# Moving three x-tile transposes behind first-piece products in the hand-written order of a 2:4-sparse linear layer

## The chip, the cores and the metric

One core of one Trainium2 chip runs the kernel. The metric is device time in microseconds (us) of one execution; lower is better. Four executions of the kernel before were timed, one of them under the profiler.

## What is computed

`x` has 16 x 512 tokens of 1024 features, `w` is 1024 x 1024, `b` has 1024 values, all bf16. The rows of `w` stand in groups of four; in each group and column the two largest magnitudes are kept and the rest set to zero. The pruned matrix multiplies all tokens, and the bias is added:

```python
    wg = w.reshape(G, M, D)
    mag = jnp.abs(wg)
    order = jnp.argsort(mag, 1)
    thr = jnp.take_along_axis(mag, order[:, M - N:M - N + 1, :], 1)
    mask = (mag >= thr)
    wp = (wg * mask).reshape(D, D)
    return jnp.einsum("bsd,df->bsf", x, wp) + b
```

## The kernel before

The 8192 tokens are 64 tiles of 128. TensorE (PE) needs, for every product, a 128 x 128 block of x with features on the partitions as weights, and up to 512 columns of the pruned matrix as the moving operand. Pruning takes VectorE (DVE) some 25 us, and the kernel is arranged so that PE has work from the first pruned columns on.

The weights are cut into six pieces (line 127): pieces 0 to 3 are 256 columns each of the upper half of the rows (g = 0), pieces 4 and 5 are 512 columns each of the lower half. In `w_sb` and `wp`, partition q holds the four rows of group q, so pruning a group is arithmetic within a partition.

The first eight tiles (0 to 7, `NPK`) use this layout as it is. Their first 512 features are loaded plainly (`load_x`, lines 116 to 122), transposed on PE with a stride of four (`transpose`, line 186), copied from PSUM to SBUF by ScalarE (ACT; `copy_xt`, line 194), and multiplied with a piece as soon as it is pruned (`mm_piece`, line 206). Two tiles of a pair (line 202) share one PSUM bank of 512 columns for each piece. When both are done, ACT copies the bank to SBUF (`stage`, line 253). Transposes rotate through two PSUM buffers (`psum_t`), partial sums through six (`psum_o`).

For everything else the pruned rows are brought back to their natural order by DMAs from `wp` to `wp_nat` (`spread`, line 141), and x arrives already transposed by transposing DMAs: `load_lead` (tiles 8 to 11), `load_low` (the second 512 features of tiles 0 to 7) and `load_nat` (all later tiles in batches). From then on PE runs products of 512 columns to the end, DVE adds the bias and ACT issues the stores.

The order of this first phase is written out by hand, one queue of tokens for each engine (`order`, line 259). A token is emitted when the tokens it needs are emitted (`needs`, `run`), and `seq` makes each engine keep the written order. So the strings in `order` are the instruction order of the engines. The tokens that matter here:

- `T3a` on PE: the four transposes of x tile 3 into a PSUM buffer (line 191, groups named `tp<-ident,x`). It wants the load of its tile and, for its buffer, the copy of the transpose two before it.
- `C3a` on ACT: the copy of that buffer to SBUF (line 196, `xt<-tp`).
- `M3.0y` on PE: the two products of tile 3 with piece 0 for the second half of the group rows (`x`: first half), line 217, `ps<-wp,xt`. Each has 256 columns. It wants `C3a` and the pruning token `mult0y`. Digits after the point are the piece.
- `S0b0` on ACT: the copy of pair 0's bank of piece 0 to `staged` (line 257, `st<-ps`). It frees a `psum_o` buffer. Pair 0 is tiles 5 and 6, pair 1 is 0 and 1, pair 2 is 2 and 3, pair 3 is 4 and 7.
- `W0.1` on SP: the DMAs that spread the pruned columns 512 to 1023 of g = 0 (line 100, `wp_nat<-wp`). `X0`, `X1`: the transposing DMAs of `xlead`.
- `A2h1` on PE: the first four products of tile 10 with columns 512 to 1023 (line 240, `ps<-wp_nat,xlead`), which want `W0.1`.

The loads of x are issued in this order: tile 7 by ACT, then by SP tiles 5 and 6, tiles 0 and 1, piece 1 of the weights, tile 4, tiles 2 and 3, and the rest of the weights. Tiles 2 and 3 are one transfer of 256 KB:

```python
    load_x(5, 7)
    load_x(0, 2)
    load_w(0, 256, 512)
    load_x(4, 5)
    load_x(2, 4)
    load_w(0, 512, 1024)
```

Of the kernel before, what the change touches and what calls it, by code (L numbers as in the profile page):

```python
# [10 lines left out]
def kernel(  # L11
# [241 lines left out]
    def stage(q, n):  # L253
        if (q, n // 2) not in staged:
# [3 lines left out]

    order = {
        "pe": (  # L260
            "F8 T7a T5a T6a T1a M5.0x M7.0x T0a M6.0x M6.0y M1.0x M7.0y M5.0y T3a M0.0y T4a M1.0y "
            "M0.0x T2a M3.0y M4.0x M3.0x M4.0y M2.0y M2.0x M4.1x M5.1x M0.1x M7.1y M6.1y M2.1y "
            "M1.1y M3.1y M6.1x M4.1y M1.1x M3.1x M0.1y M7.1x M2.1x M5.1y M0.2 M3.2 M7.2 M1.2 M2.2 "
            "M4.2 M6.2 M0.3 M2.3 M5.3 M4.3 M5.2 M6.3 M3.3 M1.3 A0h0 A2h0 M7.3 A2h1 A1h0 A3h1 A0h1 "
            "A3h0 A1h1"
        ),
        "dve": (
            "abs0a hi0a abs0b lo0a hi0b lo0b t20 t10 thr0 mask0x mult0x mask0y mult0y abs1 lo1 hi1 "
# [2 lines left out]
            "thr5 mask5 mult5"  # L271
        ),
        "act": (
            "C7a C5a C6a C1a C0a C3a C4a S0b0 C2a S3b0 S1b0 S2b0 abs3 S3b1 S1b1 S0b1 S2b1 S2b2 S1b2 "
            "S3b2 S0b2 S1b3 S2b3 W1.0q S3b3 S0b3"
        ),
        "sp": (
# [213 lines left out]
```

## Time and profile before

| | |
|---|---|
| median of the four runs | 233.75 us (233.69, 233.74, 233.76, 234.49) |
| the profiled execution | 234.49 us, of which 232.7 us is the span from first to last instruction |
| PE busy | 226.9 us, 98% of the span |
| granted clock of TensorE | 1.0 |
| transposes of x on PE (L191) | 32, 3.0 us busy |
| products of the first eight tiles with pieces 0 to 3 (L217) | 128 of 256 columns, 15.0 us busy |
| copies of transposes on ACT (L196) | 8, 0.37 us each |

The span is counted from the first instruction; times in the trace are microseconds from there. A product's recorded time (0.27 us for 256 columns) is longer than the distance to the next one, since products are pipelined. An entry such as `x4` stands for that many instructions in a row, and the bracket at the end of a line gives the idle time of the engine before it and what ended it.

### The profile page before, as it was taken

To read this page: it belongs to the slowest core of one execution; us is meant where nothing else is said; L and a number is where in the kernel's file an instruction comes from. 1 tells how busy PE (TensorE), PEld (TensorE's weight loads), DVE (VectorE), ACT (ScalarE), POOL (GpSimd) and SP (SyncE) were. 2 spreads that over 40 slices of the span, in tenths; PEclk is the share of its full clock that TensorE was granted. 3 is DMA by queue.
4 is the path that set the end of the run, shared out by engine and by line. 5 is a ranking of instruction groups with operands and counts; after the bars stand their busy time and mean duration, and the time that the engine had idled before them with its cause. 6 is when DMAs were issued, how large, how long until landed. Compare 5 with 4: busy or idle time off the path is not lost.

```text
span 232.7 us, 2829 instructions
## 1 busy us (share of the span) xinstructions
PE 226.9 (98%) x1139; PEld 112.5 (48%) x1158; DVE 108.2 (47%) x185; ACT 13.6 (6%) x27; POOL 17.6 (8%) x15
## 2 busy tenths in 40 slices
PE   8899999999999999999999999999999999999995
PEld 5688444554444444444444444444444444444443
DVE  4899858863244244234334334324324424423434
ACT  2575200000000000000000000000000000000000
POOL 1000099800000000000000000000000000000000
PEclk9999999999999999999999999999999999999999
DMA  6999999996389411992239921695228951122122
GB/s 190 300 217 227 218 183 258 310 248 236 148 186 243 157 68 70 231 285 73 90 88 216 282 92 46 155 270 162 93 90 179 238 169 68 70 90 79 60 90 90
DMA packets 78268, 38.19 MB, mean 164 GB/s; under 512 B 63664, under 2 KB 70576, under 8 KB 78256
## 3 DMA queue, kind: packets, MB, share of 16 engines
q1 hardware_dynamic: 67600, 20.88, 45.1%
q10 hardware_dynamic: 10656, 17.14, 20.7%
q8 instruction: 9, 0.15, 0.3%
q14 instruction: 3, 0.02, 0.0%
HBM read 3.41 MB, written 16.78 MB: 87 GB/s over the span
## 4 chain that ended last, share of the span: by engine, by line
PE 94%; DMA 2%; SPq 1%; issue 1%; DVE 0%
PE ps L240 87%; PE ps L217 5%; DMA x<-in_x_dram 2%; PE tp L240 1%; SPq L100 1%; PE tp L191 0%; DVE o L400 0%
## 5 line engine op out<-in xcount | busy, mean ns | idle before, releaser
L240 PE MATMUL ps<-wp_nat,xb 128*128 128x512 bf16 (+2 forms) x832 | 178.9, 375 | 0.8
L240 PEld LDWEIGHTS <-xb 128*128 128x128 bf16 x848 | 82.4, 98 | 97.5
L400 DVE TENSOR_TENSOR o<-ps,bias_sb 128x512 bf16<-128x512 f32 (+1 forms) x112 | 71.6, 677 | 114.6 <-PE ps L240 112.3
L396 POOL TENSOR_TENSOR st<-st,bias_sb 128x1024 f32<-128x1024 f32 x8 | 16.7, 2128 | 0.0
L217 PE MATMUL ps<-wp,xt 128*128 128x256 bf16 x128 | 15.0, 273 | 0.0
L240 PE MATMUL ps<-wp_nat,xlow 128*128 128x512 bf16 x62 | 14.0, 379 | 0.1
L217 PEld LDWEIGHTS <-xt 128*128 128x128 bf16 x128 | 12.3, 98 | 1.5
L402 DVE TENSOR_TENSOR o<-ps,st 128x512 bf16<-128x512 f32 x16 | 11.1, 692 | 2.8 <-PE ps L240 2.1
L240 PE MATMUL ps<-wp_nat,xlead 128*128 128x512 bf16 x47 | 11.1, 379 | 0.1
L240 PEld LDWEIGHTS <-xlow 128*128 128x128 bf16 x64 | 7.2, 112 | 6.7
L240 PEld LDWEIGHTS <-xlead 128*128 128x128 bf16 x64 | 6.3, 98 | 7.1
L257 ACT COPY st<-ps 128x512 f32<-128x512 f32 x16 | 8.5, 593 | 6.0 <-PE ps L217 4.2
L156 DVE TENSOR_TENSOR wp<-w_sb,mag 128x512 bf16<-128x512 bf16 (+2 forms) x8 | 5.4, 691 | 0.2
L156 DVE TENSOR_TENSOR mag<-mag,hi 128x512 bf16<-128x512 bf16 (+2 forms) x8 | 5.4, 690 | 0.2
L135 PE MATMUL ps<-zeros 128*128 128x128 bf16 (+1 forms) x22 | 4.2, 379 | 1.0 <-DVE zeros L86 1.0
L191 PE MATMUL tp<-ident,x 128*128 128x128 bf16 x32 | 3.0, 222 | 1.2 <-DMA x<-in_x_dram 0.9
L240 PE MATMUL tp<-wp_nat,xlead 128*128 128x512 bf16 x16 | 4.1, 379 | 0.0
L166 DVE TENSOR_SCALAR mag<-w_sb 128x512 uint16<-128x512 uint16 (+2 forms) x6 | 2.7, 467 | 2.7 <-DMA w_sb<-in_w_dram 2.7
L135 PEld LDWEIGHTS <-zeros 128*128 128x128 bf16 x22 | 2.4, 140 | 2.6 <-issue 1.6
L156 DVE TENSOR_TENSOR hi<-mag 128x512 bf16<-128x512 bf16 (+2 forms) x7 | 3.2, 460 | 0.1
L156 DVE TENSOR_TENSOR lo<-mag 128x512 bf16<-128x512 bf16 (+2 forms) x7 | 3.2, 458 | 0.0
L191 PEld LDWEIGHTS <-x 128*128 128x128 bf16 x32 | 2.3, 116 | 1.8 <-DMA x<-in_x_dram 1.4
(16 smaller groups left out, 14.0 us busy)
## 6 DMA issues: line engine op xcount, KB each, us to landing
out_dram<-o ACTq DMA_DIRECT2D x59, 256.0 KB, 2.8
wp_nat<-wp SPq DMA_DIRECT2D x14, 128.0 KB, 3.5
w_sb<-in_w_dram SPq DMA_DIRECT2D x3, 512.0 KB, 7.4
out_dram<-o ACTq DMA_DIRECT2D x8, 128.0 KB, 1.7
x<-in_x_dram SPq DMA_DIRECT2D x3, 256.0 KB, 4.2
w_sb<-in_w_dram SPq DMA_DIRECT2D x1, 256.0 KB, 4.6
bias_sb<-in_b_dram SPq DMA_DIRECT2D x1, 256.0 KB, 7.4
wp_nat<-wp ACTq DMA_DIRECT2D x2, 128.0 KB, 4.0
```

What stands on the lines that cost most here:

```text
L100: return seq(eng, q.dma_start(out_, in_))
L135: pe(nc.tensor.matmul(warm_ps[:, :rep * P], lhsT=zeros[:], rhs=zeros[:, None, :].to_broadcast([P, rep, P]), start=True, stop=True))
L156: dve(nc.vector.tensor_tensor(out, a, b_, op=op))
L166: dve(nc.vector.tensor_single_scalar(self.mag[:, ms, :].bitcast(u16), self.w[:, ms, :].bitcast(u16), 0x7FFF, op=Alu.bitwise_and))
L191: pe(nc.tensor.transpose(tp[:, m, :], xg[:, m, :], ident[:]))
L217: pe(nc.tensor.matmul(ps[:, c0 + d:c1 + d], lhsT=xpk[t][:, m, :], rhs=wp[:, g, m, c0:c1], start=(new and m == ms.start), stop=(left[(q, n) ...
L240: pe(nc.tensor.matmul(ps, lhsT=xt[:, kt - koff, :], rhs=wp_nat[:, kt, c0:c1], start=(kt == first), stop=(kt == last)))
L257: act(nc.scalar.copy(st[:, n % 2, :, :].rearrange("p t c -> p (t c)"), ps_open.pop((q, n))[:]))
L396: pool(nc.gpsimd.tensor_tensor(st[:], st[:], bias[:, :, None, :].to_broadcast([P, 2, 2, CW]), op=Alu.add))
L400: dve(nc.vector.tensor_tensor(o[:, c0:c1], ps, bias_sb[:, c0:c1], op=Alu.add))
L402: dve(nc.vector.tensor_tensor(o[:, c0:c1].rearrange("p (n c) -> p n c", n=2), ps.rearrange("p (n c) -> p n c", n=2), add, op=Alu.add))
```

## The change

Only the order of tokens changes, in the PE and the ACT queue. On PE, after `M5.0y`, the order `T3a M0.0y T4a M1.0y M0.0x T2a M3.0y M4.0x M3.0x M4.0y` becomes `M1.0y M0.0x T4a M0.0y M4.0x M4.0y T3a T2a M3.0y M3.0x`. On ACT, the copies of tiles 4 and 3 change places with the transposes, and `S0b0` goes behind `C2a`. The instructions themselves, and the queues of DVE, SP and GpSimd, are the same.

```diff
         "pe": (
-            "F8 T7a T5a T6a T1a M5.0x M7.0x T0a M6.0x M6.0y M1.0x M7.0y M5.0y T3a M0.0y T4a M1.0y "
-            "M0.0x T2a M3.0y M4.0x M3.0x M4.0y M2.0y M2.0x M4.1x M5.1x M0.1x M7.1y M6.1y M2.1y "
...
+            "F8 T7a T5a T6a T1a M5.0x M7.0x T0a M6.0x M6.0y M1.0x M7.0y M5.0y M1.0y M0.0x T4a M0.0y "
+            "M4.0x M4.0y T3a T2a M3.0y M3.0x M2.0y M2.0x M4.1x M5.1x M0.1x M7.1y M6.1y M2.1y M1.1y "
...
         "act": (
-            "C7a C5a C6a C1a C0a C3a C4a S0b0 C2a S3b0 S1b0 S2b0 abs3 S3b1 S1b1 S0b1 S2b1 S2b2 S1b2 "
+            "C7a C5a C6a C1a C0a C4a C3a C2a S0b0 S3b0 S1b0 S2b0 abs3 S3b1 S1b1 S0b1 S2b1 S2b2 S1b2 "
```

## The prediction

> **What bounds the kernel now.** I read the page first, then the chain that ended last, then the timeline of TensorE (PE) and ScalarE (ACT) around the change, and last the landing of two transfers. On the page, PE is busy 98% of the span. No other engine passes half of it, so the time is PE's own work plus the few places where it stands still.
>
> ```profile
> PE 226.9 (98%) x1139; PEld 112.5 (48%) x1158; DVE 108.2 (47%) x185; ACT 13.6 (6%) x27; POOL 17.6 (8%) x15
> PE 94%; DMA 2%; SPq 1%; issue 1%; DVE 0%
> ```
>
> The chain (start, length, what) shows where PE is not on it: SP issues, then a transfer of x, and from 9.48 us on almost only PE.
>
> ```profile
> 4.00 5.45 DMA x<-in_x_dram
> 9.44 0.04 issue
> 9.48 0.41 PE tp L191 x4
> 9.90 0.22 PE ps L217 x2
> 10.12 0.22 PE tp L191 x4
> 10.34 0.44 PE ps L217 x4
> 10.78 0.22 PE tp L191 x4
> 11.00 11.35 PE ps L217 x104
> ```
>
> So a microsecond saved or lost on PE before 11 us goes to the end, unless a later wait takes it. The timeline of PE (start, length, what) shows the stall at the edited place: T3a, the transpose of tile 3, waits for the transfer of tiles 2 and 3.
>
> ```profile
> 7.09 0.39 PE L191 MATMUL tp<-ident,x 128*128 128x128 bf16 x4
> 7.31 1.26 PE L217 MATMUL ps<-wp,xt 128*128 128x256 bf16 x10
> 9.48 0.41 PE L191 MATMUL tp<-ident,x 128*128 128x128 bf16 x4 [0.92 <-DMA x<-in_x_dram]
> 9.73 0.38 PE L217 MATMUL ps<-wp,xt 128*128 128x256 bf16 x2
> 9.95 0.39 PE L191 MATMUL tp<-ident,x 128*128 128x128 bf16 x4
> 10.18 0.60 PE L217 MATMUL ps<-wp,xt 128*128 128x256 bf16 x4
> 10.61 0.39 PE L191 MATMUL tp<-ident,x 128*128 128x128 bf16 x4
> ```
>
> ACT's timeline gives the price of turning a transpose into an operand (tile 0, whose transpose starts at 7.09, then tiles 3 and 4):
>
> ```profile
> 7.51 0.37 ACT L196 COPY xt<-tp 128x256 f32<-128x256 f32 x1 [0.29 <-PE tp L191]
> 9.94 0.82 ACT L196 COPY xt<-tp 128x256 f32<-128x256 f32 x2 [2.05 <-PE tp L191]
> 10.65 0.59 ACT L257 COPY st<-ps 128x512 f32<-128x512 f32 x1
> ```
>
> **What the Trainium skill says.** (1) "TensorE: Matmul & The Clock Gate", section "Wait — 56ns, not 53.3ns?": a warm product follows the last after its columns at 2.4 GHz plus about 2.5 ns. That gives 109 ns for 256 columns and 56 ns for 128. The trace agrees: ten products span 1.26 us, of which the last takes 0.273, so (1.26 - 0.27)/9 = 0.11; four transposes give (0.39 - 0.22)/3 = 0.056. (2) "PSUM — Partial Sum Buffer", section "Engine vs sequencer instructions": weight loads may run ahead, but products start and complete in program order. The trace agrees: M0.0y, ready since tile 0 was copied at 7.88, stood behind T3a until 9.73. So every wait that the new order makes stops all of PE. (3) "Perfetto Trace Analysis", section "DVE / Act Engine Instruction (TENSOR_ADD, Activation, etc)": an ACT window ends with the acknowledged write, and the semaphore's way comes after it. The trace has that way as short hops: tile 0's transposes end at 7.48 and the copy starts at 7.51; an earlier copy ends at 6.05 (5.68 + 0.37) and the transpose it releases starts at 6.11. (4) "DMA: Bandwidth & Descriptors", section "Latency and other measured facts": the access to HBM takes 0.2 us on average and 2 us at high load. The trace fits: tiles 2 and 3 took 5.4 us from issue to landing in a stretch in which the 16 DMA engines were busy for 0.87 of the time. How steady this is no single trace shows.
>
> **The change, part by part.** The edit moves tokens in two hand-written queues; the program has the same instructions, and SP's, VectorE's and POOL's queues are the same row for row. So nothing is added or removed but waits. Up to M5.0y both orders agree. Its second product starts at 8.29, so the next slot is 8.40.
>
> *Removed: the stall at T3a.* It starts at 9.48 in place of 8.40: 1.08 us of issue time (0.92 by the page's idle, which counts from the modelled end). Its second transpose also follows 0.03 late, as the start after a wait does. Sum: 1.11.
>
> *New order up to the first copy.* M1.0y and M0.0x (four products, operands copied by 7.88 and wp ready at 7.15) fill 8.40 to 8.84. T4a then runs at once: tile 4's own transfer was issued at 3.34 and took 4.2, so it landed at 7.54. T4a takes 4 x 0.0555 = 0.22, M0.0y another 0.22, and M4.0x could go at 9.28. But tile 4 must be copied first.
>
> *Added wait 1: M4.0x on the copy of tile 4.* For tile 0, copy end minus transpose start is 7.88 - 7.09 = 0.79; with the 0.05 hop an operand is there 0.84 after its transpose starts. From 8.84 that is 9.68, so PE stands 0.40, plus the 0.03 of a start after a wait: 0.43. Bounds: nothing in the records would shorten the chain by more than the jitter of its hops (0.03 to 0.05), so 0.38 to 0.48. In the order before, four products and T2a stood in this place and hid the copy whole. All of PE is queued behind this wait.
>
> *T3a and T2a.* M4.0x and M4.0y fill 9.71 to 10.15. T3a then starts at 10.15, 0.7 after its data landed (9.44), so the transfer is covered. T2a follows directly; it wants the PSUM buffer of tile 4, which M4.0x has already waited for. PE is free again at 10.15 + 8 x 0.0555 = 10.60.
>
> *Added wait 2: M3.0y on the copy of tile 3.* 10.15 + 0.84 = 10.99, so 0.40 and 0.03 again: 0.43, with the same bounds. Four products later M2.0y wants tile 2. Its transpose starts at 10.37 and its operand is there by 11.26 (0.84, and 0.05 because two copies in a row start at least 0.27 apart), while PE comes at 11.46. No wait.
>
> *The sum.* M4.1x, from where both orders are the same, starts at 11.90. In the order before it is twelve products after 10.84, at 12.15. Gain: 1.11 - 0.43 - 0.43 = 0.25 us.
>
> *Is the gain kept?* I went through what PE waits for next. (a) M0.1x at 12.34 takes a PSUM buffer that S0b0 empties. S0b0 now stands behind C2a: it starts about 11.11 and ends 11.70 (0.59). Cover 0.6. S3b0 follows at 0.48 steps for M2.1y at 12.99, with about 0.8 left. (b) wp of piece 1 is done on VectorE at 10.63; abs3 on ACT waits for S2b0, which comes no later than before. (c) The tight one is W0.1, the four transfers of pruned weights on SP; SP does not wait for PE here, so they do not move. The last is issued at 21.37 and takes 3.1, landing at 24.44; A2h1's fourth product wants it at 25.00 (24.35 + 3 x 0.216). So PE may come 0.56 earlier before it waits, less a hop of 0.04. The 0.25 fits, and no more than about 0.52 ever could by this trace. From 44 us on PE's products run without a gap but 0.05 us hiccups, and the tail after the last product is unchanged.
>
> ```profile
> 19.48 2.49 SPq L100 DMA_DIRECT2D wp_nat<-wp  x4
> 24.35 1.46 PE L240 MATMUL ps<-wp_nat,xlead 128*128 128x512 bf16 x6
> ```
>
> Against the profiled execution (span 232.67 and 1.82 around it, 234.49) the sum gives 234.24. That execution is the longest of the four; the median is 0.74 lower. Taking 0.25 off the median gives 233.50.
>
> **The rivals.** *Slower: the transfer is early, the copies are not.* The two waits of 0.43 depend on PE and ACT alone and are paid in every execution. The stall they replace depends on when tiles 2 and 3 land. Break-even is a landing at 9.44 - 0.25 = 9.19. The other three runs are 0.73 to 0.80 shorter than the profiled one. If all of that is this landing (8.70), the order before stalls only 0.37 and the new one takes 234.24, which is 0.49 slower than the median. With a landing by 8.40 it would be 0.86 slower, 234.61, but only if W0.1 lands earlier too, since otherwise it holds the faster order back. For it: the shorter runs. Against it: the three of them agree to 0.07 us, and the difference may as well be recording overhead.
>
> *Much faster: the transfer is usually later than in this profile.* T3a at 10.15 covers a landing up to 10.11, 0.67 later than seen, and W0.1's margin grows with the delay. Full effect: 0.25 + 0.67 = 0.92, so 232.83. Against it: the profiled execution is the long one.
>
> *Nothing.* If W0.1 lands later than here, both orders wait for it at A2h1 and the change vanishes: 233.75. The margin is 0.56, so a landing at 25.0 does it.
>
> **How the numbers follow.** Forecast (233.5, own range 233.2 to 233.7): 0.42. Slower case, 233.8 to 234.6: 0.28. Much faster, 232.8 to 233.1: 0.17. Nothing: 0.13. A measurement of this kernel tells about 0.3% from no change, which is 0.70 us: below 233.05 or above 234.45. The much faster case gives 0.14 of the first and the forecast's edge 0.02, together 0.16. Of the slower case 0.13 lies above 234.45 (a landing near 8.4, W0.1 early with it), and 0.03 goes to a chain of copies longer than its bounds: 0.16. The rest, 0.68, is within. The range of 8 in 10 takes in both rivals' full effects: 232.8 to 234.6.
>
> **What would show it.** In the new profile T3a should start near 10.15 with no wait for the transfer; T4a near 8.84; M4.0x near 9.68 and M3.0y near 10.99, both after idle time ended by ACT's copy; M4.1x near 11.90; A2h1 without a wait. I am wrong if T3a still waits for its data, if either copy wait is missing or above 0.5, if PE stands still at A2h1, or if the order before, run again, shows T3a's stall far from 0.92.

## The result, and the profile after

| | median us | runs | against the kernel before |
|---|---|---|---|
| before | 233.91 (233.35 to 235.63) | 61 | |
| changed | 234.29 (233.89 to 234.82) | 40 | ratio 1.0014, 95% interval 1.0008 to 1.0021 |

The changed kernel is 0.33 us slower (0.0014 x 233.9; 0.19 to 0.49). Forecast was 233.5, 0.25 us faster. The two spreads differ too: the shortest run of the changed kernel is 0.54 longer than the shortest of before, and its longest is 0.81 shorter.

The profiled execution of the changed kernel has a span of 233.1 us. Its page still shows PE busy nearly throughout; the waits below are new. First the page's line, then the waits (engine and line, what for, us in total, times, longest).

```profile
PE 227.2 (97%) x1139; PEld 112.5 (48%) x1158; DVE 108.2 (46%) x185; ACT 13.4 (6%) x27; POOL 17.6 (8%) x15
```

```profile
PE ps L217 <- ACT xt L196: 0.5, 2, 0.2
PE ps L240 <- DMA wp_nat<-wp: 0.5, 1, 0.5
...
PEld L217 <- DVE wp L156: 0.3, 1, 0.3
```

The timeline of PE at the edited place (start, length, what, idle time before it):

```profile
6.90 0.39 PE L191 MATMUL tp<-ident,x 128*128 128x128 bf16 x4
7.13 1.69 PE L217 MATMUL ps<-wp,xt 128*128 128x256 bf16 x14
8.65 0.39 PE L191 MATMUL tp<-ident,x 128*128 128x128 bf16 x4
8.88 0.38 PE L217 MATMUL ps<-wp,xt 128*128 128x256 bf16 x2
9.51 0.61 PE L217 MATMUL ps<-wp,xt 128*128 128x256 bf16 x4 [0.25 <-ACT xt L196]
9.95 0.61 PE L191 MATMUL tp<-ident,x 128*128 128x128 bf16 x8
10.80 2.47 PE L217 MATMUL ps<-wp,xt 128*128 128x256 bf16 x21 [0.24 <-ACT xt L196]
```

This is what the forecast described. T4a runs without a wait, M4.0x and M3.0y wait for the copies, and T3a (9.95) no longer waits for its transfer. Counted in issue time, the first wait is 9.51 - (8.88 + 2 x 0.109) = 0.41, and the second 10.80 - (9.95 + 8 x 0.0555) = 0.41. From T0a's start to M4.1x (eight products after 10.80, so 11.69) it is 4.79 us; before, it was 12.15 - 7.09 = 5.06. In these two executions the edited stretch is 0.27 us shorter, as forecast, yet the span is 0.4 longer. The rest lies elsewhere: T0a starts 0.19 earlier, M0.2 waits 0.15 for pruned weights, and PE stands still once more, far behind the edit:

```profile
35.33 0.81 PE L240 MATMUL ps<-wp_nat,xlead 128*128 128x512 bf16 x3
36.63 2.10 PE L240 MATMUL ps<-wp_nat,xlead 128*128 128x512 bf16 x9 [0.48 <-DMA wp_nat<-wp]
```

The fourth product would have come at 35.98, so 0.65 us of issue time went to the last transfer of W1.1. That sum (-0.19 - 0.27 + 0.15 + 0.65, and 0.05 in small gaps) gives the 0.4. So two single profiles tell no cause of 0.33: one has a long stall at T3a, the other a late W1.1, and the forecast's step looks right in both. The question is what the executions do that were only timed.

### The profile page after: what moved, and what is told of

The parts are those of the page before. It is cut to its first block, busy times and chain, and to the rows that moved or that the text cites. A ratio compares the mean times of both kernels' runs of the same rounds, so it can differ in the third digit from the quotient of the medians.

```text
span 233.1 us, 2829 instructions
## 1 busy us (share of the span) xinstructions
PE 227.2 (97%) x1139; PEld 112.5 (48%) x1158; DVE 108.2 (46%) x185; ACT 13.4 (6%) x27; POOL 17.6 (8%) x15
## 4 chain that ended last, share of the span: by engine, by line
PE 95%; DMA 2%; SPq 1%; issue 1%; ACT 0%; DVE 0%
PE ps L240 85%; PE ps L217 6%; PE ps L135 2%; DMA wp_nat<-wp 2%; PE tp L240 1%; SPq L100 1%; PE tp L191 1%; ACT xt L196 0%; DVE o L400 0%; DVE zeros L86 0%
## 5 line engine op out<-in xcount | busy, mean ns | idle before, releaser
L196 ACT COPY xt<-tp 128x256 f32<-128x256 f32 x8 | 2.7, 374 | 4.7 <-PE tp L191 4.7
```

Of the source, the lines that this page charges most:

```text
L196: act(nc.scalar.copy(xt[:].bitcast(fp32), xpk[t].bitcast(fp32)))
```

## The experiments

Theory A: the removed stall depends on when tiles 2 and 3 land, and in most executions that is earlier than in the profile of before, while the two copy waits are paid always. This is the slower rival of the prediction. Theory B: later transfers (W0.1, W1.1) set the time of both kernels, and the order acts only through them. Theory C: the landing scatters from execution to execution. A and C go together.

### The kernel before once more

No edit.

> The kernel before, unchanged: a second profile of it, and what the comparison gives for no change. Theory A (in executions that are only timed, x tiles 2 and 3 land near 8.9 us and not at 9.44, so the stall at T3a is about 0.5 us and not 1.1, while the two copy waits of the new order cost 0.86 always): the ratio is 1.000; a second profile may again show T3a waiting 0.7 to 1.2, since a recorded execution is longer. Theory B (a later transfer, W0.1 or W1.1, sets the time of both kernels, and the order of the transposes acts on the time only through it): ratio 1.000 too, and the profile should show PE waiting at A2h1 or at the first products of columns 512 to 1023 with the lower half of the rows. Theory C (the landing scatters from execution to execution): T3a's stall differs from 0.92 by 0.2 or more.

Ratio 1.0006 (0.9988 to 1.0024). Its timeline of PE:

```profile
7.63 1.25 PE L217 MATMUL ps<-wp,xt 128*128 128x256 bf16 x10
9.19 0.41 PE L191 MATMUL tp<-ident,x 128*128 128x128 bf16 x4 [0.31 <-DMA x<-in_x_dram]
```

The same program stalls 0.31 in place of 0.92 at T3a (0.47 of issue time in place of 1.08). The transfer landed at 9.15 in place of 9.44, and PE came to T3a 0.32 later. Theory C holds, and the stall is a difference of two moving times. The prediction had named a stall far from 0.92 as a sign that it is wrong.

Why PE comes later stands some 2 us ahead, in the transposes of tiles 7, 5, 6 and 1 (before, then before_again):

```profile
5.23 0.68 PE L191 MATMUL tp<-ident,x 128*128 128x128 bf16 x8
6.11 0.71 PE L191 MATMUL tp<-ident,x 128*128 128x128 bf16 x8 [0.20 <-ACT xt L196]
```

```profile
5.23 1.91 PE L191 MATMUL tp<-ident,x 128*128 128x128 bf16 x16
```

In before the first eight start 0.05 to 0.09 us apart, in before_again 0.107.

### The wait for the transfer taken away, in both orders

```diff
-        xg = x_sb[t].rearrange("p (q m) -> p m q", m=4)
+        xg = x_sb[{2: 6, 3: 5}.get(t, t)].rearrange("p (q m) -> p m q", m=4)
```

> The order before, but the transposes T3a and T2a read tiles 5 and 6, which are long there; the transfer of tiles 2 and 3 is still issued and landed, and nothing uses it, so those two tiles' sums are of other data. This takes away the wait for the transfer and nothing else. Theory A: faster than the kernel before by the stall that its timed executions have, 0.4 to 0.6 us (ratio 0.9975 to 0.9983). Theory B: within 0.1 us of the kernel before (0.9996 to 1.0004).

> The changed order with the same replacement (T3a and T2a read tiles 5 and 6; the sums of tiles 2 and 3 are of other data). Theory A: the transfer was covered already, so the time is that of the changed kernel, 0.3 to 0.4 us over the kernel before (1.0012 to 1.0018), and 0.86 over before_nox, or 0.5 to 0.86 if W0.1 holds before_nox back. Theory B: also like the changed kernel, and 0.3 to 0.4 over before_nox.

before_nox: 233.80, ratio 0.9989 (0.9974 to 1.0004). after_nox: 234.40, ratio 1.0018 (1.0006 to 1.0030). Without any wait for tiles 2 and 3 the changed order is 0.60 us slower than the old one, and it is no faster than in its own form. So what it pays is not the transfer. Its timeline is the changed kernel's, and both copy waits are the only ones there:

```profile
9.38 0.38 PE L217 MATMUL ps<-wp,xt 128*128 128x256 bf16 x2
10.01 0.61 PE L217 MATMUL ps<-wp,xt 128*128 128x256 bf16 x4 [0.25 <-ACT xt L196]
10.46 0.61 PE L191 MATMUL tp<-ident,x 128*128 128x128 bf16 x8
11.31 1.92 PE L217 MATMUL ps<-wp,xt 128*128 128x256 bf16 x16 [0.24 <-ACT xt L196]
```

before_nox gained less than theory A asked, 0.1 us by the medians for 0.4 to 0.6. Its profile shows a reason: PE now comes to A2h1 before W0.1 has landed.

```profile
23.05 0.81 PE L240 MATMUL ps<-wp_nat,xlead 128*128 128x512 bf16 x3
24.33 1.24 PE L240 MATMUL ps<-wp_nat,xlead 128*128 128x512 bf16 x5 [0.46 <-DMA wp_nat<-wp]
```

The fourth product of A2h1 is due at 23.70 and starts at 24.33. W0.1 is a floor under the old order when nothing else holds it, which is the part of theory B that is true. An estimate from the landings of W0.1 in the eleven profiles with this load order: it would hold before_nox by about 0.2 us on the mean, so that the two copy waits (0.41 each, 0.82 together) show as about 0.6. That is what was measured.

### One of the two waits alone

```diff
-            "... M7.0y M5.0y M1.0y M0.0x T4a M0.0y M4.0x M4.0y T3a T2a M3.0y ..."
+            "... M7.0y T4a M5.0y M1.0y M0.0x M0.0y M4.0x M4.0y T3a T2a M3.0y ..."
```

> The changed order with T4a moved ahead of four tokens, to behind M7.0y, so that eight products stand between it and M4.0x and hide the copy of tile 4; the wait of M3.0y on the copy of tile 3 stays. Theory A: 0.43 us below the changed kernel, so 0.1 us below the kernel before (ratio 0.9990 to 1.0000); its profile has M4.0x without a wait and M3.0y with one of 0.4. Theory B: like the changed kernel, 1.0012 to 1.0018.

Median 233.97, ratio 1.0003 (0.9987 to 1.0019). Its profile has one copy wait, at M3.0y:

```profile
8.88 1.47 PE L217 MATMUL ps<-wp,xt 128*128 128x256 bf16 x12
10.19 0.61 PE L191 MATMUL tp<-ident,x 128*128 128x128 bf16 x8
11.04 2.14 PE L217 MATMUL ps<-wp,xt 128*128 128x256 bf16 x18 [0.24 <-ACT xt L196]
```

By the medians it lies 0.32 below the changed kernel and 0.07 above the one before. The interval takes in both, so the direction fits theory A and the times do not settle the size. The profile does: from the start of T0a to that of M0.1x, from where all orders here run alike, it takes 4.80 us, and all four profiles with both copy waits and this load order take 5.22.

### Neither wait, and the floors behind

```diff
-            "... M7.0y M5.0y M1.0y M0.0x T4a M0.0y M4.0x M4.0y T3a T2a M3.0y M3.0x M2.0y M2.0x M4.1x M5.1x ..."
+            "... M7.0y T4a M5.0y M1.0y M0.0x M0.0y T3a M4.0x M4.0y T2a M3.0y M3.0x M4.1x M5.1x M2.0y M2.0x ..."
```

> An order with neither wait: T4a behind M7.0y, T3a behind M0.0y, T2a behind M4.0y, and M4.1x M5.1x ahead of M2.0y, so that at least four products stand between each transpose and its first product. Theory A (copy waits against the landing): PE does the first phase without either cost, 0.86 us ahead of the changed order. If nothing later holds PE, 233.1 to 233.5 us (ratio 0.997 to 0.9985). If the transfer W0.1 is a floor, as in the profile of before_nox, where PE stood 0.46 us at A2h1, it stops near before_nox, 233.7 to 233.9 (0.999 to 1.000), and its profile shows PE waiting for wp_nat at A2h1. Theory B (only later transfers count): like the kernel before.

234.04 by the median, ratio 0.9996 (0.9985 to 1.0006): better than the changed kernel, and not told from the one before. Its profile has no wait of PE for a copy or for the transfer, and a span of 232.0, as short as that of before_nox. One small wait is new: M4.1x, moved ahead, is due at 10.85 and starts at 11.04, when VectorE has finished the first half of piece 1 (11.00). It did not wait at A2h1 in that execution, though the margin was small: the fourth product came at 24.33 and W0.1 landed at 24.20.

The next two, the old and the changed order, move only the place at that floor: `A2h1 A1h0 A3h1 A0h1 A3h0 A1h1` becomes `A1h0 A3h0 A2h1 A3h1 A0h1 A1h1`.

> The order before, with the products of columns 512 to 1023 of the lead tiles moved behind those of columns 0 to 511 (A1h0 and A3h0 ahead of A2h1), so that W0.1 has 1.7 us more. If W0.1 holds the kernel before in the executions where tiles 2 and 3 are early, this gains what it held: 0.1 to 0.3 us (ratio 0.9987 to 0.9996). If W0.1 is never late for it: 1.000.

> The changed order with the same move of A1h0 and A3h0. The changed order comes to A2h1 after W0.1 in all three profiles that have it, so by theory A nothing is gained: like the changed kernel, 1.0012 to 1.0018 over the kernel before, and 0.4 to 0.6 us over before_h1late. Theory B (W0.1 is what holds both): as fast as before_h1late.

before_h1late: ratio 1.0005 (0.9995 to 1.0016). after_h1late: 1.0020 (1.0011 to 1.0029). The move gains nothing that shows for either; for the old order the interval leaves at most about 0.1 us. So W0.1 does not make the difference of the two kernels, and theory B falls as far as W0.1 goes: with it out of the way the changed order is still 0.15% slower. (W1.1 is not moved here; the late transfer below speaks against theory B as a whole.) For the old order this is no surprise afterwards, since in its two profiles PE's stall at T3a had already put A2h1 behind W0.1.

> The order of hidden, with A1h0 and A3h0 ahead of A2h1, and the closing products of tiles 4 and 0 (columns 0 to 511) ahead of those of columns 512 to 1023, which gives W1.1 1.7 us more as well. If W0.1 and W1.1 are the floors that keep the first phase's gain from the end, this is the fastest: 233.1 to 233.5 us (0.997 to 0.9985). If the landing and the copies decide nothing: within 0.1 us of the kernel before.

233.78, ratio 0.9989 (0.9981 to 0.9998), so 0.26 us faster than the kernel before and by the medians 0.5 faster than the changed one. It is the only version computing the same result that is told from the kernel before, and narrowly. It was expected to gain 0.4 us and more. Its interval, 0.05 to 0.44 us, takes in the 0.39 that the old order's stall comes to on the mean (see the table below), so no part of the gain need be missing. Its profile (span 232.0) names no wait of PE behind the first filler, and no gap over 0.05 us from T0a on; the phase ahead was slow in it, with T0a only at 7.51. How much of the gain comes from the moved floors is not shown, since this version is not told from hidden.

### The transfer later, in both orders

```diff
-    load_x(2, 4)
     load_w(0, 512, 1024)
+    load_x(2, 4)
```

> The order before, with the transfer of tiles 2 and 3 issued behind the weights of columns 512 to 1023, so that it lands later, at an estimated 10.3 to 11.2 us (it has 0.5 MB more ahead of it). Theory A (the change trades a stall that depends on this landing against two copy waits of 0.41 that do not): T3a stands still for 1.8 to 2.6 us in place of 0.43 on the mean, so this is 1.3 to 2.2 us over the kernel before (ratio 1.0055 to 1.0095), less what the earlier weights give back at W0.1. Theory B (later transfers alone decide): within 0.3 us of the kernel before.

> The changed order with the same late transfer. Its T3a comes at about 10.1 and waits only for what is beyond that. Theory A: the sign turns: 0.25 to 0.3 us faster than before_late, by 1.11 to 1.15 of later slot less 0.41, 0.41 of copies (the first copy wait stays, the second stays too), while at the usual landing the same edit is 0.33 us slower. Theory B: as slow against before_late as the changed kernel is against the kernel before, by 0.3 us.

before_late: 237.1, ratio 1.0118 (1.0077 to 1.0159). after_late: 235.06, ratio 1.0048 (1.0032 to 1.0064). Theory B's forecast, within 0.3 us of the kernel before, fails. The sign turns: with the late transfer the changed order is the faster one, so the same edit costs or gains by when tiles 2 and 3 land. Behind M0.1x the weights that were moved forward act on neither profile: from there to the end both take 220.1 us, as nearly all others do. One stall each shows it, first before_late, then after_late:

```profile
10.09 0.41 PE L191 MATMUL tp<-ident,x 128*128 128x128 bf16 x4 [1.72 <-DMA x<-in_x_dram]
```

```profile
9.44 0.61 PE L217 MATMUL ps<-wp,xt 128*128 128x256 bf16 x4 [0.24 <-ACT xt L196]
10.96 0.64 PE L191 MATMUL tp<-ident,x 128*128 128x128 bf16 x8 [0.91 <-DMA x<-in_x_dram]
11.84 2.36 PE L217 MATMUL ps<-wp,xt 128*128 128x256 bf16 x20 [0.24 <-ACT xt L196]
```

The size of after_late's expectation was worked out wrong: T3a stands 1.74 us later in the new order than in the old (3.05 after T0a's start in place of 1.31), less two copy waits of 0.41 is 0.92, not 0.25. Measured: 0.60 between the means of the executions at full clock, eight of before_late and its repeat (235.82) and 17 of after_late (235.22). Their scatter leaves the size open, from about 0.2 to 1.0 (95%, by resampling the executions). The rest of the distance between the medians is a second effect, seen next.

> before_late once more, unchanged: in 3 of its 6 executions the mean granted clock was 0.993 and the time 237.7 to 238.1, in the other 3 it was 1.0 and 235.1 to 236.5. Theory D (a stall of about 2 us or more at T3a is at times followed by a stretch at half clock): 0.7% of 236 us is 1.65 us of lost clock, a stretch of 3.3 us at half rate, so about half of the executions should again be near 0.993 and some 2 us longer than the others, with nothing between; a profile that catches one shows products at twice their distance right after T3a. Theory E (the landing is simply later in those executions): the times scatter without two groups, and the clock does not go with them.

Median 236.11, ratio 1.0100 (1.0068 to 1.0132). One of six executions was at clock 0.993 (238.22), five at 1.0 (235.22 to 236.20). Of the twelve executions of this kernel, the four at 0.993 took 237.74 to 238.22 and the eight at 1.0 took 235.08 to 236.46, with nothing between. Two groups that go with the clock: theory D fits, E does not, though one of six is fewer than the half that D expected. The 17 executions of after_late, whose profile stalls 1.08 at T3a, were all at 0.999 or 1.0. No profile caught one of the four, so that the lost clock follows the stall is argued from the size and not shown.

### The changed kernel once more

> The changed kernel, unchanged, in one call with the others and with the kernel before: ratio 1.0008 to 1.0021, and a further profile. Theory A: again two copy waits of 0.40 to 0.42 us, T3a without a wait if tiles 2 and 3 land before about 10.1. If the wait for W1.1 of 0.65 us in its first profile is a rule and not that one execution, PE stands still at the same product again.

234.40, ratio 1.0017 (1.0007 to 1.0027). Its profile has both copy waits again, and no other wait of PE after its first filler:

```profile
PE ps L135 <- DVE zeros L86: 1.0, 1, 1.0
PE ps L217 <- ACT xt L196: 0.5, 2, 0.2
```

So the 0.65 us at W1.1 belonged to that one execution; no other profile shows it.

## Why the prediction was wrong

**The step that failed** is the first term of the sum: "Removed: the stall at T3a ... Sum: 1.11". The two waits that the edit adds, 0.82 together, are more than the stall that it takes away in nine of the eleven rows below. The stall was read off one execution and then taken as the stall of the median run. Its size is the landing of tiles 2 and 3 minus the moment PE comes to T3a, and both move. Eleven profiles have the loads in the original order. In each, T0a's start plus 1.31 is when the old order would come to T3a:

| profile | T0a starts | old order at T3a | tiles 2, 3 land | old order's stall |
|---|---|---|---|---|
| before | 7.09 | 8.40 | 9.44 | 1.08 |
| changed | 6.90 | 8.21 | 9.62 | 1.45 |
| before_again | 7.41 | 8.72 | 9.15 | 0.47 |
| before_nox | 6.78 | 8.09 | 8.02 | 0 |
| after_nox | 7.41 | 8.72 | 8.16 | 0 |
| one_wait | 7.56 | 8.87 | 8.48 | 0 |
| hidden | 7.34 | 8.65 | 8.92 | 0.31 |
| before_h1late | 7.41 | 8.72 | 9.45 | 0.78 |
| after_h1late | 7.02 | 8.33 | 8.47 | 0.18 |
| hidden_h1close | 7.51 | 8.82 | 8.63 | 0 |
| after_again | 7.41 | 8.72 | 8.65 | 0 |

(The stall counts 0.04 from landing to start. It was measured in before, before_again and before_h1late; in the others it is worked out for an order that they did not run.) The mean is 0.39 in place of 1.08, with the 0.03 of a late second transpose only where there is a stall. With the copy waits as they were measured, the sum is 0.82 - 0.39 = 0.43 us slower; with the 0.63 that W0.1 costs in the row of before_nox it is 0.37. The chip says 0.33 (0.19 to 0.49), so the timed runs ask for a mean stall of about 0.49. The sample is small: the three measured stalls average 0.78, the eight worked out 0.24. Nothing ahead of T3a differs in the loads of these programs, so this is taken as scatter, which is not shown.

Both times move. Against the profile of before, the mean landing of the eleven is 0.62 earlier (8.82) and the mean start of T0a 0.17 later (7.26). T0a goes with the spacing of the early matmuls: in the four profiles in which it drops from 0.107 to 0.055 us before 5.1 us, T0a starts at 6.78 to 7.09, in the seven in which it drops after 5.9 us, at 7.34 to 7.56.

The spans leave no room for another cause in the profiles. From M0.1x to the end it takes 220.09 to 220.10 us in nine of the eleven. In the other two it takes as much more as their later waits: 220.85 in before_nox (0.63 at A2h1, 0.11 for pruned weights) and 220.96 in the first profile of the changed kernel (0.65, 0.15 and 0.05). From T0a to M0.1x the old order takes 4.39 plus its stall and that 0.03, the changed order 5.22.

**The added waits** were right: 0.43 each forecast, 0.40 to 0.41 in every profile that has them. (Six products and T2a, not four, stood between T4a and M4.0x in the order before; nothing in the sum rests on it.) The same holds for the gain in an execution like the profiled one: 0.25 forecast, 0.27 between the two profiles.

**The rival** "the transfer is early, the copies are not" was the case. It named the break-even landing, and its 234.24 is near what came out (234.29). It is right in the mechanism; that the number fits so well is in part luck, since it held PE's arrival fixed and laid all of the shorter runs to the landing. Its case was given 0.28 although three runs of four, all 0.7 shorter than the profiled one, spoke for it. That they agree to 0.07 us was taken against it; four runs are too few for that, since the 61 now known scatter over 2.3 us. The other objection, that the profiled run was long by its recording, explains little: the eleven profiled executions in the table lie 0.17 us above the median of their kernel on the mean, and two of them 0.25 and 0.37 below.

**The floor W0.1** was sized rightly (0.52 to 0.56 of margin in that profile) and shows in before_nox at the product named. It decided little here. The two other rivals, much faster and nothing, did not occur; that a late transfer turns the sign is what before_late and after_late showed.

**The range** (232.8 to 234.6) holds the time, and the change is within 0.3% as the likeliest case had it. The sign was not. The narrower spread of the changed kernel fits the cause: it has no stall that comes and goes with a landing before about 10, and it can't have the short runs without any stall.

## What to carry to other kernels

A stall that ends with a DMA's landing is a sample of a scattering quantity: before trading it for a wait that is fixed, look at a second profile, or take away the wait by reading other data, and compare the fixed cost with the mean of the stall and not with the one seen. A copy between two engines costs its whole latency (0.85 to 0.86 us here, from the first transpose to the first product) unless that much other work stands between; put such work there rather than moving the producer behind it. A gain early in a stream is worth only what the next transfers leave of it, as before_nox shows at A2h1; hidden_h1close moves those places too, though what that adds is not shown.

## What the runs showed of the hardware

The landing of one 256 KB transfer, issued at 3.98 to 4.00 us in the eleven profiles above, lay between 8.02 and 9.62. The profiles come from more than one chip; the four of before_again, before_nox, after_nox and one_wait, all from one, still lie between 8.02 and 9.15. "DMA: Bandwidth & Descriptors" in the Trainium skill, section "Latency and other measured facts", lets the access to HBM vary with load; these programs carry the same load up to there, and the scatter is 1.6 us all the same. The 5.4 us that the prediction set beside that section's figures are the whole time from issue to landing behind other loads, so they do not test them (and the DMA share of that stretch, 4.00 to 9.44, is 0.92; 0.87 is that of 8.20 to 9.60).

Four of twelve executions with a late transfer ran at a mean granted clock of 0.993 and took 2.2 us more (means 238.03 and 235.82). In 0.7% of 236 us, 1.65 us of clock is lost, as much as 3.3 us at half rate. "TensorE: Matmul & The Clock Gate" in the Trainium skill, section "What's actually happening", has TensorE fall to half clock after an idle window of about 3.4 us. The stalls that profiles of this kernel show are 1.7 to 1.9 us at full clock; how long they were in the four executions was not seen, so no run here shows whether that section applies. Of the kernel before, 167 executions with a recorded clock stand beside the experiments, and one of them was such (235.95, clock 0.993); of the changed kernel's 62 none was.
